# The last sums by pairs of experts, turned logits first, the last weight block in pieces, and the output's remainders in two transfers

## The chip, the cores and the metric

The kernel runs on one core of one Trainium2 chip. The metric is the time of one execution on the device, in microseconds (us); the figure for a kernel is the median of its runs. A profile shows one such execution: its span from the first instruction to the last, on TensorE (PE; its weight loads are PEld), VectorE (DVE), ScalarE (ACT), GpSimd (POOL) and SyncE (SP), whose queue issues nearly all transfers. The 16 DMA engines of the core move the data.

## The reference

Attention through a memory of 32 slots for each of 4 sequences and 8 heads, then a dense mixture of 4 experts, then a soft mixture of 8 experts with 4 slots each. The last part is where the change lies:

```python
def _moe_ref(x, domain_probs, w1, w2):
    p = domain_probs / (domain_probs.sum(-1, keepdims=True) + 1e-09)
    for e in range(E):                       # 4 experts, F = 1024
        h = np.maximum(x @ w1[e], 0.0)
        out += p[:, e:e + 1] * (h @ w2[e])

def _moe2_ref(x, phi, w1, w2):               # x: 2304 tokens x 512
    logits = x @ phi                         # 2304 x 32 slots
    d = np.exp(logits - logits.max(0)); d /= d.sum(0) + 1e-09
    slot_input = (d.T @ x).reshape(8, 4, 512)
    for e in range(8):                       # F = 1024
        h = np.maximum(slot_input[e] @ w1[e], 0.0)
        slot_out[e] = h @ w2[e]
    c = np.exp(logits - logits.max(1)); c /= c.sum(1) + 1e-09
    return c @ slot_out                      # 2304 x 512
```

## The kernel before

**The token part.** The 2304 tokens are worked in five units: three sequences of 576 tokens whole, the fourth in two halves of 288. In each unit `up` makes the hidden values of the four experts, 128 at a time, with three passes of matmuls (L767 to L769); ACT applies the relu (L776) into a ring of buffers `hts`, DVE turns them (L782), POOL multiplies them by the expert's share (L786). They stay in a large buffer `h` with regions R[0] to R[4] of 4608 words; in the last unit experts 0 and 1 lie in R[0] and experts 2 and 3 in R[1]. `w2` is not applied to tokens: the logits come from hidden values and a product `M` of `w2` and `phi` (L805, L812), and the slots' sums are taken over hidden values and multiplied by `w2` afterwards.

**The group behind each unit** (`group`). A matmul folds the four row groups of the logits (L922; in the last unit a second, L926). ACT copies the result from its PSUM bank to `lr` (L930, kept for the softmax over slots) and DVE turns the same bank into `lc` (L937). `lc` gives the running maximum (L946), the exponential (L951) and, turned back, `dt` (L957). Then the sums (L975): for each block `tb` of 32 tokens (9 in the last unit), each of the two pairs of experts `ep`, and each of four row groups `p`, one matmul with 32 rows, 32 columns and 512 streamed values. Its place in the array is row group `p` and column group `c = 2 * (tb % 2) + ep`; row group `p` writes bank `S0 + p`. Each fp32 matmul is two instructions, so the last unit has 72 matmuls in 144 instructions. DVE then adds them to the running sums, `srun` (L995).

**The end.** `srun` is turned (L1204), multiplied by the four `w2` (L1235), folded (L1249), and goes through the slot experts' `v1` (L1278) and `v2` (L1322). These weights are 40 blocks of 1 MB, `loads`: 8 of `w2`, 16 of `v1`, 16 of `v2`. Each gets a home in a part of a buffer that is no longer used (`homes`, 21 of them, in turn); the first 21 are issued as their homes come free, the other 19 each behind the block that held its home before. Five of the homes overlap R[0] and R[1], and two the buffers `hts`. SP issues them in program order, one at a time: an issue whose home is still read holds back all behind it. Each transfer also waits for the landing of the eighth before it. `load_block` issues a block as one transfer, or as two of 512 KB where its home has two parts.

The `v2` products of a half of the experts lie in one bank `ab`, in four column groups `kk`, 16 rows each. When the last block has been used, ACT and DVE copy the bank's halves (L1337, L1339), a matmul each (L1343) folds the four groups into banks `bf`, ACT and DVE copy these to `so4` (L1347, L1349), and `result` makes the output: matmuls (L1361), copies by DVE and ACT in turn (L1367, L1370), and transfers by SP (L365). The 64 tokens of each sequence beyond 512, its remainder, go out in four transfers of 128 KB from POOL's queue.

**The order.** Every step is handed to a planner with an engine, an estimated cost, what it reads and writes, and a due time `at`. The planner lists the steps of each engine in the order in which it believes they can start; that list is the program. Dependences and the waits for them are found per instruction when the program is built. Two engines' reads of one PSUM bank wait for one another, in program order.

## Time and profile before

| | us |
|---|---|
| median of 3 runs | 506.42 |
| lowest and highest run | 505.79, 507.36 |
| the profiled execution | 505.81 |
| its span, first to last instruction | 504.0 |
| PE busy in the span | 472.2 |
| DVE, ACT, POOL busy | 297.5, 202.4, 214.7 |

The granted TensorE clock is full up to the last microseconds (0.992 on average). PE is busy nearly without gaps from about 50 to 410 us. Behind that, in the last 94 us, the stages are short and have different limits: the DMA engines' share of time, the chain through PE, DVE and ACT, and SP's waits have to be read stage by stage, by windows of the trace and by the timeline. SP's waits are told with what released them, and a share of DMA time of 1 means that all 16 engines moved data throughout.

### The profile page before, as it was taken

To read this page: it belongs to the slowest core of one execution; us is meant where nothing else is said; L and a number is where in the kernel's file an instruction comes from. 1 tells how busy PE (TensorE), PEld (TensorE's weight loads), DVE (VectorE), ACT (ScalarE), POOL (GpSimd) and SP (SyncE) were. 2 spreads that over 40 slices of the span, in tenths; PEclk is the share of its full clock that TensorE was granted. 3 is DMA by queue.
4 is the path that set the end of the run, shared out by engine and by line. 5 is a ranking of instruction groups with operands and counts; after the bars stand their busy time and mean duration, and the time that the engine had idled before them with its cause. 6 is when DMAs were issued, how large, how long until landed. Compare 5 with 4: busy or idle time off the path is not lost.

```text
span 504.0 us, 13235 instructions
## 1 busy us (share of the span) xinstructions
PE 472.2 (94%) x5596; PEld 339.2 (67%) x5596; DVE 297.5 (59%) x606; ACT 202.4 (40%) x476; POOL 214.7 (43%) x259
## 2 busy tenths in 40 slices
PE   3889999999999999999999999999999989999880
PEld 2677678787886788788768887866697866332230
DVE  6588546657675958767875676685667553110041
ACT  2354345555551455455334655543452430010031
POOL 0244133646652347785315578643674950000001
PEclk9999999999999999999999999999999999999996
DMA  7999956416430847362073734643436998999948
GB/s 223 219 350 301 366 146 213 164 31 189 132 120 3 283 118 223 107 189 83 3 228 110 220 125 164 201 142 126 168 97 223 360 345 309 413 426 420 420 167 287
DMA packets 65403, 106.08 MB, mean 210 GB/s; under 512 B 28608, under 2 KB 40896, under 8 KB 59712
## 3 DMA queue, kind: packets, MB, share of 16 engines
q1 hardware_dynamic: 65152, 104.71, 61.3%
q8 instruction: 44, 0.72, 0.6%
q0 software_dynamic: 192, 0.52, 0.5%
q14 instruction: 15, 0.12, 0.1%
HBM read 100.50 MB, written 4.72 MB: 209 GB/s over the span
## 4 chain that ended last, share of the span: by engine, by line
PE 84%; DMA 7%; DVE 3%; SPq 2%; ACT 1%; issue 0%; DVEq 0%; ACTq 0%
PE ps L767 15%; PE ps L769 13%; PE ps L768 13%; PE ps L975 8%; PE ps L692 6%; PE ps L805 5%; DMA h<-in_moe_w_dram 5%; PE ps L1278 4%; PE ps L836 3%; SPq L365 2%; PE ps L600 2%; PE ps L612 2%; PE ps L1322 2%; PE ps L812 2%; PE ps L853 2%; DMA h<-in_q_dram 2%
## 5 line engine op out<-in xcount | busy, mean ns | idle before, releaser
L786 POOL TENSOR_TENSOR h<-h,pe 128x576 f32<-128x576 f32 (+1 forms) x160 | 158.0, 995 | 138.5 <-DVE h L782 108.4
L767 PE MATMUL ps<-A,g 128*128 128x288 f32 x512 | 157.9, 308 | 0.0
L776 ACT ACTIVATE hts<-ps 128x288 f32<-128x288 f32 x256 | 105.2, 412 | 130.6 <-PE ps L769 129.2
L769 PE MATMUL ps<-A,g 128*128 128x288 f32 x512 | 151.5, 296 | 0.2 <-DVE g L703 0.2
L768 PE MATMUL ps<-A,g 128*128 128x288 f32 x512 | 151.2, 295 | 0.0
L782 DVE STREAM_TRANSPOSE h<-hts 128x576 f32<-128x576 f32 (+1 forms) x160 | 102.8, 648 | 51.3 <-ACT hts L776 50.8
L767 PEld LDWEIGHTS ps<-A,g 128*128 128x128 f32 x512 | 96.3, 188 | 22.5 <-issue 14.2
L769 PEld LDWEIGHTS ps<-A,g 128*128 128x128 f32 x512 | 96.2, 188 | 0.9 <-DVE g L703 0.9
L768 PEld LDWEIGHTS ps<-A,g 128*128 128x128 f32 x512 | 96.4, 188 | 0.1
L703 DVE TENSOR_TENSOR g<-ps,g 128x512 fp32r<-128x512 f32 x64 | 41.0, 678 | 17.8 <-ACT g L701 17.7
L701 ACT CAST g<-ps 128x512 fp32r<-128x512 f32 x64 | 34.9, 590 | 33.8 <-PE ps L692 33.1
L975 PE MATMUL ps<-h,dts 32*32 32x512 f32 x1152 | 40.0, 597 | 1.6 <-DVE dts L957 1.6
L365 POOL DMA_DIRECT2D out_dram<-v x4 | 2.3, 568 | 80.2 <-ACT v L1370 80.2
L692 PE MATMUL ps<-raw,vbs 64*32 64x512 f32 x512 | 35.0, 601 | 1.3 <-DVE small L636 1.3
L975 PEld LDWEIGHTS ps<-h,dts 32*32 32x32 f32 x1152 | 22.8, 103 | 15.2 <-issue 4.7
L805 PE MATMUL ps<-hts,M 128*32 128x288 f32 x384 | 28.2, 411 | 0.0
L629 POOL TENSOR_TENSOR atts<-atts,small 128x256 f32<-128x256 f32 (+1 forms) x20 | 11.4, 572 | 25.2 <-DVE small L627 25.1
L836 PE MATMUL ps<-ident,h 128*128 128x128 f32 x128 | 18.1, 278 | 1.1 <-DMA h<-in_moe_w_dram 1.1
L805 PEld LDWEIGHTS ps<-hts,M 128*32 128x32 f32 x384 | 10.4, 109 | 10.6 <-issue 5.1
L640 POOL TENSOR_TENSOR atts<-atts,small 128x256 f32<-128x256 f32 (+1 forms) x20 | 11.5, 573 | 13.0 <-DVE small L638 5.5
L836 PEld LDWEIGHTS ps<-ident,h 128*128 128x128 f32 x128 | 14.5, 143 | 3.4 <-DVE h L782 1.4
L893 POOL TENSOR_TENSOR lts<-lts,pe 128x288 f32<-128x288 f32 x15 | 10.3, 688 | 13.0 <-DMA v<-in_moe_w_dram 9.6
(186 smaller groups left out, 519.0 us busy)
## 6 DMA issues: line engine op xcount, KB each, us to landing
raw<-in_moe_w_dram SPq DMA_DIRECT2D x32, 1024.0 KB, 5.3
v<-in_moe_w_dram SPq DMA_DIRECT2D x20, 1024.0 KB, 11.7
h<-in_moe_w_dram SPq DMA_DIRECT2D x18, 1024.0 KB, 8.2
h<-in_k_dram SPq DMA_DIRECT2D x8, 512.0 KB, 5.1
h<-in_v_dram SPq DMA_DIRECT2D x8, 512.0 KB, 6.5
atts<-in_moe_w_dram SPq DMA_DIRECT2D x4, 1024.0 KB, 9.2
atts<-in_q_dram SPq DMA_DIRECT2D x12, 256.0 KB, 5.7
atts<-in_phi_dram SPq DMA_DIRECT2D x8, 256.0 KB, 4.8
```

What stands on the lines that cost most here:

```text
L692: nc.tensor.matmul(bank[bs[c]][32 * i:32 * i + 32, :], vb[b % 2][64 * c:64 * c + 64, 32 * i:32 * i + 32], t()[64 * c:64 * c + 64, i, :], s ...
L701: add(ACT, act(512), lambda c=c, src=src: nc.scalar.copy(out=placed(g()[:, 2 * c]), in_=src), r=[pk(bs[c])], w=[wk(o + 1024 * c, 512)], at ...
L703: add(DVE, dve(512), lambda c=c, src=src: nc.vector.tensor_tensor(out=placed(g()[:, 2 * c + 1]), in0=src, in1=placed(g()[:, 2 * c].bitcast ...
L767: nc.tensor.matmul(t, gh, ah, start=(c == 0), stop=False)
L768: nc.tensor.matmul(t, gh, al, start=False, stop=False)
L769: nc.tensor.matmul(t, gl, ah, start=False, stop=(c == 1))
L776: add(ACT, act(w), lambda: nc.scalar.activation(out=t[:, o0 - base:o1 - base], in_=bank[bm][:, 0:w], func=ACTF.Relu,), r=[pk(bm)], w=[wk(h ...
L782: add(DVE, dve(width), lambda: nc.vector.transpose(out=h_of(u, e)[:, kx], in_=t), r=[wk(ho, width)], w=[hk], at=at + 0.4)
L786: add(POOL, pool(width), lambda: nc.gpsimd.tensor_tensor(out=h_of(u, e)[:, kx], in0=h_of(u, e)[:, kx], in1=share, op=ALU.mult), r=["pe"], ...
L805: nc.tensor.matmul(lb[r0:r0 + 32, 0:HB], M[:, 4 * n + a, :], at_place(hos[a] + o0, o1 - o0), start=(first and h == 0), stop=(not first and ...
L836: nc.tensor.transpose(bank[bk][:, 128 * c:128 * c + 128], wn()[:, a, 128 * c:128 * c + 128], ident)
L975: nc.tensor.matmul(bank[S0 + p][32 * c:32 * c + 32, :], dtv[rows, tb, :], h_pair(u, ep)[rows, :, :, tb, :], start=(tb < 2), stop=(tb >= nt ...
```

## The change

Six edits. (1) In every unit, DVE's turning of the folded logits into `lc` is put ahead of ACT's copy of them to `lr`. (2) In the last unit the sums run over all token blocks for experts 0 and 1 first and then for experts 2 and 3, where they took both pairs block by block; `c` keeps its formula. A home in R[0] so hangs on the first pair alone. (3) The last eight matmuls of the last unit's logits become seven and one. (4) The last `v2` block is issued in three transfers, of 512, 256 and 256 KB. Its last 128 rows are no longer multiplied into `ab` but, with a new 128-wide table `hl` that holds the hidden values of expert 7 at the columns of its slots four times over, straight into the banks `bf`, ahead of the fold. `hl` lies in the share table `pe`; POOL clears it and DVE fills it. (5) The output's remainders go out from SP in two transfers of 256 KB, two sequences each. (6) Some estimated costs and due times change with them.

```diff
@@ logits
-                for m, ho in enumerate(hos):
+                for m in ms:
...
-        add(PE, 1.1, f,
-            r=[("M", m) for m in range(n0, n + 1)] + [wk(o, width) for o in hos], w=[pk(LB)], at=at, lag=0)
+        last = u == NU - 1 and n == NCH - 1
+        for ms in (range(7), range(7, 8)) if last else (range(8),):
+            add(PE, 0.15 * len(ms) if last else 1.1, lambda ms=ms: f(ms),
...
@@ group
-        for ki, bk in enumerate((b1, b2)[:len(ranges)]):
-            add(ACT, act(HB), lambda ki=ki, bk=bk: nc.scalar.copy(
-                out=lr[:, HB * ki:HB * ki + HB], in_=bank[bk][:, 0:HB],
-            ), r=[pk(bk)], w=["lr"], at=at[0] + 0.1)
...
             add(DVE, dve(HB), lambda ki=ki, bk=bk: nc.vector.transpose(
                 out=lc[:, HB * ki:HB * ki + HB], in_=bank[bk][:, 0:HB],
             ), r=[pk(bk)], w=["lc"], at=at[0] + 0.1)
+        for ki, bk in enumerate((b1, b2)[:len(ranges)]):
+            add(ACT, act(HB), lambda ki=ki, bk=bk: nc.scalar.copy(
+                out=lr[:, HB * ki:HB * ki + HB], in_=bank[bk][:, 0:HB],
+            ), r=[pk(bk)], w=["lr"], at=at[0] + 0.2)
...
-        def sums(tbs):
+        def sums(tbs, eps):
             for tb in tbs:
-                for ep in range(2):
+                for ep in eps:
                     c = 2 * (tb % 2) + ep
                     for p in range(4):
...
-        for t0 in range(0, nt, 2):
...
+        for eps in ((0,), (1,)) if final else ((0, 1),):
+            ks = [hks[e] for e in range(E) if e // 2 in eps]
+            for t0 in range(0, nt, 2):
+                tbs = range(t0, min(t0 + 2, nt))
+                add(PE, 0.43 * len(tbs) + 0.02, lambda tbs=tbs, eps=eps: sums(tbs, eps), r=["dt"] + ks, w=sb, at=at[3])
@@ load_block
+            for a, z in ((0, 2), (2, 3), (3, 4)) if m == len(loads) - 1 else ((0, n),):
+                dma(
+                    lambda t=t, a=a, z=z, n=n: t() if z - a == n else t()[:, a:z],
+                    src if z - a == n else src[:, a:z], 262144 * (z - a), w=[wk(o + 512 * a, 512 * (z - a))],
...
@@ the end
+    hl = pe.rearrange("p b n e -> p (b n e)")[:, 0:128].rearrange("p (c s) -> p c s", c=4)
+    add(POOL, 0.3, lambda: nc.gpsimd.memset(hl, 0.0), w=["pe"], at=z4 + 2.4)
...
+            if m == 3:
+                nc.vector.tensor_copy(
+                    out=hl[:, :, 28:32], in_=tv[:, 1, 1, 3, 28:32].unsqueeze(1).to_broadcast([128, 4, 4])
+                )
...
+            for kks in ((0, 1), (2,)) if last else (range(4),):
+                add(PE, 0.15 * len(kks), lambda kks=kks, f=f: f(kks),
+                    r=[tk[kk] for kk in kks] + [("hz", e // 2)], w=[pk(ab)], at=at + 0.001 * kks[0])
...
         for h, cs in enumerate(halves):
+            if n:
+                add(PE, 0.45, lambda h=h, cs=cs, t=t: nc.tensor.matmul(
+                    bank[bf[h]][:, 0:256], hl.rearrange("p c s -> p (c s)"), t(3)[:, cs], start=False, stop=False,
+                ), r=[tk[3], "pe"], w=[pk(bf[h])], at=at + 0.09 + 0.1 * h)
             add(PE, 0.35, lambda n=n, h=h, so=so, fold=fold, cs=cs: nc.tensor.matmul(
...
-                dma(
-                    out[b * S + 512:b * S + 576, :], lambda t=t, b=b, rows_out=rows_out: t()[rows_out, b // 2, :],
-                    131072, r=[k_], w=[wk(o + 512 * b, 512)], at=at + 0.05, cost=1.0, eng=POOL,
-                )
                 at += 0.1
+                if b % 2:
+                    dma(
+                        out.rearrange("(b s) d -> b s d", b=B)[b - 1:b + 1, 512:576, :],
+                        lambda t=t, b=b: t()[:, b // 2, :], 262144, r=[k_, ("tail", b - 1)],
...
```

How this moves instructions, at three places. First SP's queue where the homes in `hts` and in R[0] and R[1] are loaded (`h_89` is that buffer; 128x2048 is a block of 1 MB, 128x1024 half of one; a wait names the engines or the transfers waited for). Before:

```order
L365 DMA hts<-in_moe_w_dram 128x2048 [waits DMAHW2_49,DVE_49,PE_49]
L365 DMA hts<-in_moe_w_dram 128x1024 [waits DMAHW3_49]
L365 DMA h_89<-in_moe_w_dram 128x1024 [waits DMAHW4_49,PE_49,Pool_49]
L365 DMA h_89<-in_moe_w_dram 128x2048 [waits DMAHW5_49]
L365 DMA h_89<-in_moe_w_dram 128x2048 [waits DMAHW6_49]
L365 DMA h_89<-in_moe_w_dram 128x2048 [waits DMAHW7_49]
L365 DMA h_89<-in_moe_w_dram 128x2048 [waits DMAHW0_49]
L365 DMA atts<-in_moe_w_dram 128x2048 [waits DMAHW1_49,PE_49]
```

And now:

```order
L365 DMA hts<-in_moe_w_dram 128x1024 [waits DMAHW2_49,DVE_49,PE_49]
L365 DMA hts<-in_moe_w_dram 128x2048 [waits DMAHW3_49,DVE_49,PE_49]
L365 DMA h_89<-in_moe_w_dram 128x2048 [waits DMAHW4_49,PE_49,Pool_49]
L365 DMA h_89<-in_moe_w_dram 128x2048 [waits DMAHW5_49,Pool_49]
L365 DMA h_89<-in_moe_w_dram 128x1024 [waits DMAHW6_49,PE_49,Pool_49]
L365 DMA h_89<-in_moe_w_dram 128x2048 [waits DMAHW7_49]
L365 DMA h_89<-in_moe_w_dram 128x2048 [waits DMAHW0_49]
L365 DMA atts<-in_moe_w_dram 128x2048 [waits DMAHW1_49,PE_49]
```

Two whole blocks, which wait for PE's first pair of experts, now stand ahead of the half block, which waits for the second pair.

Second, PE from the last `v2` block to the first results (L1322 and now L1340 are the `v2` matmuls, L1343 and now L1368 the folds). Before:

```order
L1322 MATMUL ps_92<-h_89,vbs 16x512 [waits DMAHW5_49]
L1322 MATMUL ps_92<-h_89,vbs 16x512 x3
L1343 MATMUL ps_99<-lrs,r_69 128x256 [waits Activation_49]
L1343 MATMUL ps_98<-lrs,r_69 128x256 [waits DVE_49]
L1361 MATMUL ps_93<-kbs,ct 128x256 [waits Activation_49]
L1361 MATMUL ps_94<-kbs,ct 128x256
L1361 MATMUL ps_95<-kbs,ct 128x256 [waits DVE_49]
```

And now:

```order
L1340 MATMUL ps_92<-h_89,vbs 16x512 [waits DMAHW5_49]
L1340 MATMUL ps_92<-h_89,vbs 16x512
L1340 MATMUL ps_92<-h_89,vbs 16x512 [waits DMAHW6_49]
L1365 MATMUL ps_99<-h_89,pe 128x256 [waits DMAHW7_49,Pool_49]
L1368 MATMUL ps_99<-lrs,r_69 128x256 [waits Activation_49]
L1365 MATMUL ps_98<-h_89,pe 128x256
L1368 MATMUL ps_98<-lrs,r_69 128x256 [waits DVE_49]
L1386 MATMUL ps_93<-kbs,ct 128x256 [waits Activation_49]
L1386 MATMUL ps_94<-kbs,ct 128x256
L1386 MATMUL ps_95<-kbs,ct 128x256 [waits DVE_49]
```

The block's four matmuls are now three, behind two transfers, and the third transfer is waited for by the first of two new matmuls, one ahead of each fold.

Third, SP's queue at the output. Before (the remainders are in POOL's queue):

```order
L365 DMA out_dram<-atts 128x1024 [waits DMAHW1_49,Activation_49]
L365 DMA out_dram<-h_89 128x512 [waits DMAHW2_49,DVE_49]
L365 DMA out_dram<-h_89 128x512 [waits DMAHW3_49,Activation_49]
L365 DMA out_dram<-h_89 128x1024 [waits DMAHW4_49,Activation_49]
L365 DMA out_dram<-h_89 128x1024 [waits DMAHW5_49,DVE_49]
L365 DMA out_dram<-atts 128x1024 [waits DMAHW6_49,Activation_49]
```

And now:

```order
L365 DMA out_dram<-atts 128x1024 [waits DMAHW3_49,Activation_49]
L365 DMA out_dram<-h_89 128x512 [waits DMAHW4_49,DVE_49]
L365 DMA out_dram<-h_89 128x512 [waits DMAHW5_49,Activation_49]
L365 DMA out_dram<-v 2x64x512 [waits DMAHW6_49,DVE_49,Activation_49]
L365 DMA out_dram<-v 2x64x512 [waits DMAHW7_49,DVE_49,Activation_49]
L365 DMA out_dram<-h_89 128x1024 [waits DMAHW0_49,DVE_49]
```

The two remainder transfers stand ahead of the last four of SP's transfers. At the split of the logits' last eight matmuls the order of PE's instructions is the same as before.

## Rows read from the trace of the kernel before

**Rows 1.** The page: mean busy share of the 16 DMA engines, 40 slices of 12.6 us.

```profile
DMA  7999956416430847362073734643436998999948
```

**Rows 2.** Windows behind the sums: stretch, its length, each engine's busy us (instructions), clock, DMA share, GB/s.

```profile
419.00:420.00 1.00, 1.00 (x30) 0.31 (x10) 0.00 (x0) 0.00 (x0) 0.00 (x0) 1.00 0.22 78
420.00:421.00 1.00, 1.00 (x12) 0.72 (x8) 0.67 (x2) 0.00 (x0) 0.00 (x0) 1.00 0.00 0
421.00:422.00 1.00, 0.81 (x8) 0.57 (x6) 1.00 (x4) 0.00 (x0) 0.00 (x0) 1.00 0.45 66
422.00:423.00 1.00, 0.56 (x5) 0.57 (x6) 1.00 (x3) 0.00 (x0) 0.00 (x0) 1.00 0.83 188
```

**Rows 3.** Timeline, 412 to 430: start us, us, engine, line, tiles, count [idle before <-releaser].

```profile
412.08 0.40 ACT L930 COPY lrs<-ps 128x288 f32<-128x288 f32 x1 [3.17 <-PE ps L926]
412.51 0.48 DVE L937 STREAM_TRANSPOSE lcs<-ps 128x288 f32<-128x288 f32 x1 [1.27 <-ACT lrs L930]
...
414.96 5.39 PE L975 MATMUL ps<-h,dts 32*32 32x512 f32 x144 [1.60 <-DVE dts L957]
...
420.49 2.63 SPq L365 DMA_DIRECT2D h<-in_moe_w_dram  x5
...
427.28 2.01 SPq L365 DMA_DIRECT2D atts<-in_moe_w_dram  x3
```

**Rows 4.** Windows of line L975 alone, start of its 144 instructions: PE, PEld busy us.

```profile
414.90:415.10 0.20, 0.14 (x16) 0.14 (x31) 1.00 0.77 328
```

**Rows 5.** Timeline of ACT and DVE at the third unit's group.

```profile
330.40 1.07 ACT L701 CAST g<-ps 128x512 fp32r<-128x512 f32 x2 [0.38 <-PE ps L692]
...
329.75 0.85 DVE L937 STREAM_TRANSPOSE lcs<-ps 128x288 f32<-128x288 f32 x2
...
331.55 1.28 DVE L703 TENSOR_TENSOR g<-ps,g 128x512 fp32r<-128x512 f32 x2
```

**Rows 6.** Timeline of PE at the `v2` blocks of experts 4 to 7.

```profile
467.29 1.05 PE L1322 MATMUL ps<-v,h 128*16 128x512 f32 x8
...
468.87 1.05 PE L1322 MATMUL ps<-v,h 128*16 128x512 f32 x8
...
480.71 1.05 PE L1322 MATMUL ps<-h,vbs 128*16 128x512 f32 x8 [0.86 <-DMA h<-in_moe_w_dram]
```

**Rows 7.** Timeline from the last block to the first and last outputs.

```profile
483.15 1.05 PE L1322 MATMUL ps<-h,vbs 128*16 128x512 f32 x8 [0.80 <-DMA h<-in_moe_w_dram]
484.27 0.37 ACT L1337 COPY lrs<-ps 128x256 f32<-128x256 f32 x1 [18.12 <-PE ps L1322]
484.68 0.42 DVE L1339 COPY lrs<-ps 128x256 f32<-128x256 f32 x1 [18.07 <-ACT lrs L1337]
...
484.69 1.16 PE L1343 MATMUL ps<-lrs,r 128*128 128x256 f32 x4 [0.49 <-ACT lrs L1337]
...
485.43 0.37 ACT L1347 COPY kbs<-ps 128x256 f32<-128x256 f32 x1 [0.79 <-PE ps L1343]
...
485.89 0.42 DVE L1349 COPY kbs<-ps 128x256 f32<-128x256 f32 x1 [0.79 <-PE ps L1343]
...
487.54 1.29 SPq L365 DMA_DIRECT2D out_dram<-h  x2
...
494.40 3.77 SPq L365 DMA_DIRECT2D out_dram<-atts  x2
```

**Rows 8.** Transfers by queue from 488 to 493: packets, MB, share of 16 engines.

```profile
q1 hardware_dynamic: 637, 1.70, 88.1%
```

**Rows 9.** The same from 493 to 499; POOL's transfers are the software queue.

```profile
q0 software_dynamic: 191, 0.52, 41.5%
```

**Rows 10.** Windows: loads of 512 KB, then the end of the output (columns as above).

```profile
473.00:477.00 4.00, 2.97 (x23) 1.03 (x24) 0.00 (x0) 0.00 (x0) 0.00 (x0) 1.00 1.03 419
...
501.00:502.00 1.00, 0.00 (x0) 0.00 (x0) 0.00 (x0) 0.00 (x0) 0.00 (x0) 0.50 0.68 279
502.00:503.00 1.00, 0.00 (x0) 0.00 (x0) 0.00 (x0) 0.00 (x0) 0.00 (x0) 0.50 0.13 53
```

More of the change, by code (lines that the diff above doesn't have):

```diff
@@ L796, in logits, with f @@
         hos = [ht_of[u, m, a] for m in range(n0, n + 1) for a in range(4)]
-        def f():
+        def f(ms=range(8)):
             if len(ranges) == 2:
@@ L810, in f @@
             else:
-                for m, ho in enumerate(hos):
+                for m in ms:
                     nc.tensor.matmul(
-                        lb[32 * (m % 4):32 * (m % 4) + 32, 0:HB], M[:, 4 * n0 + m, :], at_place(ho, HB),
+                        lb[32 * (m % 4):32 * (m % 4) + 32, 0:HB], M[:, 4 * n0 + m, :], at_place(hos[m], HB),
                         start=m < 4, stop=m >= 4,
@@ L816, in logits @@
         width = ranges[-1][1] - base
-        add(PE, 1.1, f,
-            r=[("M", m) for m in range(n0, n + 1)] + [wk(o, width) for o in hos], w=[pk(LB)], at=at, lag=0)
+        last = u == NU - 1 and n == NCH - 1
+        for ms in (range(7), range(7, 8)) if last else (range(8),):
+            add(PE, 0.15 * len(ms) if last else 1.1, lambda ms=ms: f(ms),
+                r=[("M", m) for m in range(n0, n + 1)] + [wk(o, width) for o in (hos[ms[0]:ms[-1] + 1] if last else hos)],
+                w=[pk(LB)], at=at + (0.01 * ms[0] if last else 0), lag=0)
     def m_chunk(n, ats):
@@ L978, in sums @@
                         )
-        for t0 in range(0, nt, 2):
-            tbs = range(t0, min(t0 + 2, nt))
-            add(PE, 0.43 * len(tbs) + 0.02, lambda tbs=tbs: sums(tbs), r=["dt"] + hks, w=sb, at=at[3])
+        for eps in ((0,), (1,)) if final else ((0, 1),):
[3 more added lines that the diff above has]
+                add(PE, 0.43 * len(tbs) + 0.02, lambda tbs=tbs, eps=eps: sums(tbs, eps), r=["dt"] + ks, w=sb, at=at[3])
         for p in range(4):
@@ L1305, in spread_h @@
                 )
-        add(DVE, 0.5, spread_h, r=[pk(bt)], w=[("hz", m)] + hzs[m][1], at=zz + 2.6)
+            if m == 3:
+                nc.vector.tensor_copy(
+                    out=hl[:, :, 28:32], in_=tv[:, 1, 1, 3, 28:32].unsqueeze(1).to_broadcast([128, 4, 4])
+                )
+        add(DVE, 0.6, spread_h, r=[pk(bt)], w=[("hz", m)] + hzs[m][1] + (["pe"] if m == 3 else []), at=zz + 2.6)
     so4 = kbs.rearrange("p n c x -> p (n c x)")
@@ L1318, in program, with f @@
             ab = accs[e // 4]
-            def f(e=e, nn=nn, t=t, ab=ab):
-                for kk in range(4):
+            last = (e, nn) == (7, 1)
+            def f(kks, e=e, nn=nn, t=t, ab=ab):
+                for kk in kks:
                     nc.tensor.matmul(
-                        bank[ab][32 * kk:32 * kk + 16, :], hz(e, nn, kk), t(kk),
-                        start=(e % 4 == 0 and nn == 0), stop=(e % 4 == 3 and nn == 1),
+                        bank[ab][32 * kk:32 * kk + 16, :], hz(e, nn, kk), t(kk), start=(e % 4 == 0 and nn == 0),
+                        stop=(e == 3 and nn == 1) or (e == 7 and nn == (0 if kk == 3 else 1)),
                     )
             at = zz + 0.1 * (2 * e + nn)
-            add(PE, 0.6, f, r=tk + [("hz", e // 2)], w=[pk(ab)], at=at)
+            for kks in ((0, 1), (2,)) if last else (range(4),):
+                add(PE, 0.15 * len(kks), lambda kks=kks, f=f: f(kks),
+                    r=[tk[kk] for kk in kks] + [("hz", e // 2)], w=[pk(ab)], at=at + 0.001 * kks[0])
             refill(at + 0.05)
@@ L1341, in program @@
         fold = (rr, r1)[n].rearrange("p i s -> p (i s)")
+        t, tk = blk[2, 7, 1]
         for h, cs in enumerate(halves):
+            if n:
+                add(PE, 0.45, lambda h=h, cs=cs, t=t: nc.tensor.matmul(
+                    bank[bf[h]][:, 0:256], hl.rearrange("p c s -> p (c s)"), t(3)[:, cs], start=False, stop=False,
+                ), r=[tk[3], "pe"], w=[pk(bf[h])], at=at + 0.09 + 0.1 * h)
             add(PE, 0.35, lambda n=n, h=h, so=so, fold=fold, cs=cs: nc.tensor.matmul(
@@ L1390, in program @@
                 )
-                dma(
-                    out[b * S + 512:b * S + 576, :], lambda t=t, b=b, rows_out=rows_out: t()[rows_out, b // 2, :],
-                    131072, r=[k_], w=[wk(o + 512 * b, 512)], at=at + 0.05, cost=1.0, eng=POOL,
-                )
                 at += 0.1
+                if b % 2:
+                    dma(
+                        out.rearrange("(b s) d -> b s d", b=B)[b - 1:b + 1, 512:576, :],
+                        lambda t=t, b=b: t()[:, b // 2, :], 262144, r=[k_, ("tail", b - 1)],
+                        w=[wk(o + 512 * (b // 2), 512)], at=at,
+                    )
             continue
```

2 lines of the change are left out of this document (1 added, 1 removed).

## Prediction

> **What bounds the kernel now.** I read the page's slices first, then windows of the last hundred microseconds, then the timeline at the places the change touches. The DMA engines are near full from the 32nd slice on, with an 8 in the 34th (415.8 to 428.4) and 4 and 8 in the last two [rows 1]. The reader should see two things in the windows behind the last token sums: DMA falls to 0.22, 0, 0.45 and 0.83 of full in four microseconds, 2.5 us of engine time lost [rows 2], and SP issues five loads at 420.49, right where the sums end, 414.96 + 5.39 = 420.35 [rows 3]. From there to the last weight block the engines are full, so what starts the loads sooner should end them sooner. PE does not set that end: it waits about 0.8 us for each of the last blocks, which come every 2.44 us (480.71, then 483.15), although it can do one in 1.58 us [rows 6, 7]. Behind the last block a chain of matmul, copies and folds runs 4.39 us to the first output [rows 7], and then 4.7 MB go out. So three stretches can pay: the hole, the chain, the output.
>
> **Turned logits first.** ACT's copy starts at 412.08 and DVE's turn of the same bank at 412.51 [rows 3]. With the turn first, everything from there to the sums comes 0.43 us sooner: -0.4. ACT's copy then lies beside DVE's next steps. In the four earlier groups ACT now waits for DVE. At the third unit DVE reaches the turns at 329.75 and does two in 0.85; ACT was free for its casts at 330.02 and got their matmuls at 330.40 [rows 5]. Now its second copy ends about 331.0, and the casts, queued behind it, come 0.6 later. The first, half of 1.07 and a little, ends at 331.6, where DVE wanted it at 331.55 [rows 5], and PE waits for DVE. That is 0.05. The other groups have no cast behind the copy. I take +0.1 and keep 0 to 0.7, one whole shift, for the range.
>
> **The sums by pairs.** The first 16 instructions run at once [rows 4]: each matmul has its own place, row group `p` and column group `c`. Two token blocks with both pairs fill the 16 places, so nine blocks are four and a half rounds, five turns of 5.39 / 5 = 1.08 us [rows 3]. One pair has only columns 0 and 2, or 1 and 3: eight places. Is a round of eight shorter? The nearest row is a `v2` block, a lone round of four places, and it takes 1.05 us [rows 6]: a round costs the same however many places it fills. So the first pair's nine blocks are again five turns, 5.39 us, and end no sooner than both pairs do now. The second pair's first two blocks can go beside the first pair's last one (other columns); its other seven take four turns more. The sums take 5.39 + 4 x 1.08 = 9.7 us. The other bound is 5.39, with the first pair done in half of it; I take 9.7, since four places and sixteen agree. No row shows whether a matmul may pass one that waits for its place. The Trainium skill (TensorE: Matmul & The Clock Gate, the mechanism of packing small matmuls) says that matmuls start and end strictly in program order; by that the turns add up as here, and without it the sum would be 5.39.
>
> What follows: the sums start at 414.53 and the first pair ends at 419.92, so the two whole blocks are issued at 420.06, where five loads were at 420.49. The gain is the 0.4 already counted, and the hole shrinks by that alone. The second pair ends at 424.23, so SP holds the half block, and all behind it, until 424.4. The two blocks are 2.1 MB, 5.0 us at 419 GB/s [rows 10], from about 421.3, so they last to 426.3; data follow an issue by 1 to 2 us (420.49 to the window 421 to 422 [rows 2, 3]). That is just in time. The next refills are released by PE's work on `w2`, at 427.28 [rows 3], 6.93 behind the sums; they move to 431.2, data by 432.2 to 433.2, and the 2.5 blocks ahead of them last to 432.5. PE as a whole is 3.9 us late. It catches up where it waits: from the block at 467.29 to that at 480.71 are six blocks in 13.42 us, which at 1.58 take 9.48 [rows 6], room for 3.94. All three fit with little to spare: +0.1, range 0 to 1.5.
>
> **The last block in pieces.** Bytes are the same. Rows become 4 and 2 KB; the nearest price is the output, 16 x 5 x 0.881 / 1.70 = 41.5 engine-us per MB [rows 8], against 16 x 1.03 / 0.419 = 39.3 for loads of half blocks [rows 10]: 0.5 MB of it is 0.07 us. Take +0.1. Call T the time at which PE sees the last landing, 483.15 now. Now ACT copies at T + 1.12, the folds' results are copied at T + 2.28 (ACT) and T + 2.74 (DVE), the first output starts at T + 4.39 [rows 7]. Then: the second piece lands 256 KB / 419 GB/s = 0.63 ahead, its matmul is through at T - 0.63 + 1.12 = T + 0.49, ACT's half is copied at T + 0.86 and DVE's, after it, at T + 1.32. On PE a matmul of 256 columns takes some 0.43 of the 1.16 for two folds with their drain. The new matmul runs before ACT is done, the first fold starts at T + 0.88, the second new matmul at 1.31, the second fold at 1.74. A copy follows 0.74 behind the start of its fold (484.69 to 485.43 [rows 7]): T + 1.62 and T + 2.48. The output needs both halves, and so comes 2.74 - 2.48 = 0.26 sooner. Net -0.2, range -0.5 to +0.2.
>
> **The remainders.** POOL's four transfers, 0.52 MB, took 41.5% of 16 engines for 6 us, 39.8 engine-us [rows 9]. At SP's price of 41.5 per MB the same bytes cost 21.6. The engines were full, so 18.2 / 16 = 1.1 us go. At the end they finish unevenly: 0.68 and 0.13 of full in the last two microseconds [rows 10], so they would end together 1.0 sooner than the last does. I take half of that as POOL's doing, where packets of two prices share the engines: -1.6 in all, range 0 to -2.1. SP's two more issues are hidden as long as the engines are behind it; they are, since the last issue begins near 496.3 and the end is over 6 us later [rows 7, 10].
>
> **At nothing.** The logits' split leaves PE's order as it was. The table's clearing is POOL's last step, the fill one small copy on DVE ahead of an idle stretch of 18 us [rows 7]; if that cover went, each would cost a few tenths.
>
> The sum: -0.4 + 0.1 + 0.1 - 0.2 - 1.6 = -2.0. The profiled execution took 505.81 (span 504.0 and 1.8 around it), so 503.8; it lies 0.6 below the median of the runs, 506.42, which gives 504.4.
>
> **The rivals.** (a) *The first pair frees its home early.* A round of eight places takes half a turn, the pair ends at 414.53 + 2.7 = 417.2, before the queue runs dry, and the hole of 2.5 goes whole. For it: the diff orders it so. Against it: the lone round of four [rows 6]. It gives 504.4 - 2.2 = 502.2. (b) *The longer sums are not covered.* The refills come 0.7 late, PE is 0.4 late at the last block, the casts cost 0.4: 505.9, no difference. For it: all margins are a few tenths. (c) *SP becomes the bound of the output.* Its last two issues took 1.9 us each [rows 7]; if that is their own price and not the engines' back-pressure, two more eat the 1.6: 506.0. (d) *The pieces pay one by one.* If each of the two further pieces began only when the one ahead had landed, each would add the way from issue to data, up to 1.9 us: 504.4 + 3.8 = 508.2, slower. It decides from 1.8 us a piece. Against it: halves of blocks in the same queue keep 419 GB/s [rows 10]. The Trainium skill (DMA: Bandwidth & Descriptors, the bandwidth measured by size) asks for transfers of 1 MiB and more, with about 2 us fixed in each; by that it would be 4.0 and 508.4, and rows 10 speak against it for transfers that queue behind others.
>
> **How the numbers follow.** Forecast 0.55, spread 503.4 to 505.4; (a) 0.10; (b) 0.20; (c) 0.08; (d) 0.07. Measurement can tell 0.3%, 1.5 us, from no change: faster means below 504.9. About four fifths of the forecast, all of (a) and a little of (b) lie there: 0.56. The rest of the forecast, (b) and (c) make 0.37, (d) 0.07. The range 502.1 to 506.1 leaves out (d) and the edges.
>
> **What would show it.** Right: the 144 instructions of the sums take near 9.7 us, the five loads start near 420.1, 420.5 and then 424.4; DMA's hole stays about 2 us; PE waits again for the last two blocks; the first output comes near T + 4.1; no software queue, and an even end of the output. Wrong: sums of 5.4 us, or loads issued before 418 (rival a); a second dip near 426 or 432, or PE without a wait for the last block (b); output with DMA below full before its end (c); a gap between the last three landings (d).

## The result, and the profile after

The changed kernel takes 513.75 us (median of 4 runs, 513.18 to 515.36) against 506.11 (4 runs, 505.04 to 507.36): 1.0147 times as long, 95% interval 1.0117 to 1.0176. I had forecast 504.4 and given slower a chance of 0.07, by another mechanism. The profiled execution took 515.36, with a span of 513.6. Executions differ from one another in their first 30 us, while the first inputs land, so I read stages from a row inside the kernel: here line L767 first runs at 32.3, in the kernel before at 29.5, and its last instruction is at 409.6 and 407.9.

Up to the output nothing was lost. The timeline from the last fold of the logits to the refills (line numbers have moved: L926 is L929, L937 is L936, L930 is L940, L975 is L978, L1322 is L1340):

```profile
412.95 0.75 PE L929 MATMUL ps<-lts,rr 128*128 128x288 f32 x2 [0.42 <-DVE lts L896]
...
413.74 0.48 DVE L936 STREAM_TRANSPOSE lcs<-ps 128x288 f32<-128x288 f32 x1 [0.84 <-PE ps L929]
414.26 0.40 ACT L940 COPY lrs<-ps 128x288 f32<-128x288 f32 x1 [3.68 <-DVE lcs L936]
...
416.19 7.39 PE L978 MATMUL ps<-h,dts 32*32 32x512 f32 x144 [1.17 <-DVE dts L960]
...
420.78 4.24 SPq L365 DMA_DIRECT2D h<-in_moe_w_dram  x5
...
430.51 1.19 SPq L365 DMA_DIRECT2D atts<-in_moe_w_dram  x2
```

DVE turns before ACT copies. The sums take 7.39 us where they took 5.39, and SP issues the first load 4.59 behind their start, where it was 5.53 [rows 3]. Only the two whole blocks come sooner. The half block and the two loads behind it wait for PE's second pair, as the prediction had said: the third of the five is issued at 423.72, 7.53 behind the start of the sums, where in the kernel before it is at 421.35, 6.39 behind. Both issues, the changed kernel's first, and the changed kernel's wait for them on SP between 421.5 and 426 (us, times, longest):

```profile
423.72 0.33 SPq L365 DMA_DIRECT2D h<-in_moe_w_dram  x1
421.35 0.42 SPq L365 DMA_DIRECT2D h<-in_moe_w_dram  x1
SPq L365 <- PE ps L978: 1.4, 1, 1.4
```

The DMA hole is shallow now; to compare with [rows 2] (columns as there):

```profile
420.00:421.00 1.00, 1.00 (x36) 0.43 (x25) 0.00 (x0) 0.00 (x0) 0.00 (x0) 1.00 0.90 369
421.00:422.00 1.00, 1.00 (x25) 0.55 (x17) 0.00 (x0) 0.00 (x0) 0.00 (x0) 1.00 0.61 123
422.00:423.00 1.00, 1.00 (x31) 0.47 (x15) 0.00 (x0) 0.00 (x0) 0.00 (x0) 1.00 0.75 188
423.00:424.00 1.00, 1.00 (x18) 0.49 (x5) 0.43 (x2) 0.00 (x0) 0.00 (x0) 1.00 0.79 319
```

That is 0.95 us of engine time lost in four microseconds instead of 2.5. The timeline from the last block to the output, against [rows 7]:

```profile
483.36 1.32 PE L1340 MATMUL ps<-h,vbs 128*16 128x512 f32 x6
484.61 0.70 PE L1365 MATMUL ps<-h,pe 128*128 128x256 f32 x2
...
486.74 0.42 DVE L1374 COPY kbs<-ps 128x256 f32<-128x256 f32 x1 [1.20 <-PE ps L1368]
...
488.40 1.57 SPq L365 DMA_DIRECT2D out_dram<-h  x2
490.06 0.88 SPq L365 DMA_DIRECT2D out_dram<-atts  x2
491.03 2.18 SPq L365 DMA_DIRECT2D out_dram<-h  x2
493.31 1.47 SPq L365 DMA_DIRECT2D out_dram<-v  x2
494.88 5.20 SPq L365 DMA_DIRECT2D out_dram<-h  x2
500.17 1.61 SPq L365 DMA_DIRECT2D out_dram<-atts  x2
```

Counted from the last fold, the first output starts at 75.45 (412.95 to 488.40), where it was 76.25: 0.8 sooner. The fold in the kernel before:

```profile
411.29 0.75 PE L926 MATMUL ps<-lts,rr 128*128 128x288 f32 x2 [0.43 <-DVE lts L893]
```

The loss begins behind the first output. Windows of the output:

```profile
490.00:495.00 5.00, 3.30 (x24) 1.20 (x16) 4.34 (x8) 3.58 (x7) 0.00 (x0) 1.00 0.93 359
495.00:500.00 5.00, 0.00 (x0) 0.00 (x0) 0.00 (x0) 0.00 (x0) 0.00 (x0) 0.52 0.44 135
500.00:505.00 5.00, 0.00 (x0) 0.00 (x0) 0.00 (x0) 0.00 (x0) 0.00 (x0) 0.50 0.87 322
505.00:512.00 7.00, 0.00 (x0) 0.00 (x0) 0.00 (x0) 0.00 (x0) 0.00 (x0) 0.50 0.14 55
```

For the last seven microseconds the DMA engines are busy to 0.14, at 55 GB/s. Of 16 engines two are 0.125. Behind the first output SP's longest wait is now the landing of the last one, at the end of the program (us, times, longest):

```profile
SPq L1458 <- DMA out_dram<-atts: 10.7, 1, 10.7
```

The remainders (`out_dram<-v`, 493.31) are the only new thing there. Their pattern on the output's side is 2 sequences x 64 rows x 512, the two sequences outermost, and on the side of SBUF 128 partitions.

### The profile page after: what moved, and what is told of

Read it like the earlier page. It is cut to its first block, busy times and chain, and to the rows that moved or that the text cites. A ratio compares the mean times of both kernels' runs of the same rounds, so it can differ in the third digit from the quotient of the medians.

```text
span 513.6 us, 13246 instructions
## 1 busy us (share of the span) xinstructions
PE 478.0 (93%) x5598; PEld 341.7 (67%) x5598; DVE 297.6 (58%) x607; ACT 202.6 (39%) x476; POOL 212.6 (41%) x256
## 4 chain that ended last, share of the span: by engine, by line
PE 85%; DMA 6%; DVE 2%; SPq 1%; ACT 1%; issue 0%; DVEq 0%; ACTq 0%
PE ps L767 15%; PE ps L769 13%; PE ps L768 13%; PE ps L978 8%; PE ps L692 6%; PE ps L805 5%; PE ps L1290 4%; DMA h<-in_moe_w_dram 3%; PE ps L839 3%; PE ps L600 2%; PE ps L612 2%; DMA h<-in_q_dram 2%; PE ps L812 2%; PE ps L856 2%; SPq L365 1%; PE ps L1245 1%
## 5 line engine op out<-in xcount | busy, mean ns | idle before, releaser
L767 PE MATMUL ps<-A,g 128*128 128x288 f32 x512 | 157.8, 308 | 0.0
L767 PEld LDWEIGHTS ps<-A,g 128*128 128x128 f32 x512 | 96.3, 188 | 22.5 <-issue 14.2
L978 PE MATMUL ps<-h,dts 32*32 32x512 f32 x1152 | 42.0, 596 | 1.2 <-DVE dts L960 1.2
L978 PEld LDWEIGHTS ps<-h,dts 32*32 32x32 f32 x1152 | 23.3, 103 | 16.2 <-issue 6.8
L839 PEld LDWEIGHTS ps<-ident,h 128*128 128x128 f32 x128 | 14.6, 143 | 2.1 <-issue 0.9
L654 POOL TENSOR_TENSOR A<-atts,A 128x256 fp32r<-128x256 f32 (+1 forms) x20 | 13.6, 678 | 4.4 <-ACT A L652 4.4
```

The lines of the kernel that those rows point to most:

```text
L767: nc.tensor.matmul(t, gh, ah, start=(c == 0), stop=False)
L839: nc.tensor.transpose(bank[bk][:, 128 * c:128 * c + 128], wn()[:, a, 128 * c:128 * c + 128], ident)
L978: nc.tensor.matmul(bank[S0 + p][32 * c:32 * c + 32, :], dtv[rows, tb, :], h_pair(u, ep)[rows, :, :, tb, :], start=(tb < 2), stop=(tb >= nt ...
```

## The experiments

"First load" and "first output" are counted from the start of the last unit's sums; "output" is from SP's first issue to the last packet; all four are of the profiled execution. A ratio is to runs of the kernel before that were taken beside that kernel's, with medians between 505.65 and 506.11, so it does not follow from the column of times. The last unit's steps up to the output are the same in changed, a_pool, a_tokens and a_one2, and their first outputs still lie between 71.4 and 72.2; c_adj, which differs in one column number, has 72.7. So a difference of less than about 1 us in that column tells nothing. l_copyfirst's is late by an event told below.

| kernel | us | ratio to before (95%) | sums | first load | first output | output |
|---|---|---|---|---|---|---|
| before | 506.11 | 1 | 5.39 | 5.53 | 72.6 | 15.2 |
| changed | 513.75 | 1.0147 (1.0117 to 1.0176) | 7.39 | 4.59 | 72.2 | 23.8 |
| a_pool | 505.83 | 1.0008 (0.9981 to 1.0035) | 7.39 | 4.59 | 72.0 | 15.1 |
| a_tokens | 504.89 | 0.9971 (0.9947 to 0.9995) | 7.39 | 4.60 | 71.4 | 14.6 |
| a_one2 | 510.08 | 1.0099 (1.0063 to 1.0136) | 7.39 | 4.59 | 72.0 | 19.3 |
| b_two2 | 514.21 | 1.0165 (1.0149 to 1.0180) | 5.39 | 5.54 | 73.1 | 23.5 |
| l_oldsums | 504.94 | 0.9971 (0.9958 to 0.9985) | 5.39 | 5.54 | 72.5 | 14.6 |
| l_oneblock | 505.13 | 0.9991 (0.9968 to 1.0013) | 7.39 | 4.59 | 72.3 | 14.8 |
| l_copyfirst | 505.02 | 0.9992 (0.9971 to 1.0013) | 7.39 | 4.59 | 73.1 | 14.5 |
| b_tokens | 505.97 | 0.9996 (0.9985 to 1.0007) | 5.39 | 5.53 | 72.6 | 14.6 |
| c_adj | 505.17 | 0.9993 (0.9981 to 1.0004) | 7.39 | 4.59 | 72.7 | 14.6 |
| c_four | 503.04, one run | | 5.98 | 3.27 | 70.7 | 14.5 |
| s_skew2 | 505.18 | 0.9990 (0.9974 to 1.0007) | 6.05 | 5.18 | 73.0 | 14.5 |
| s_skew4 | 505.08 | 0.9984 (0.9969 to 0.9999) | 6.71 | 4.99 | 72.2 | 14.8 |

### Where the loss lies

**a_pool** takes the fifth edit back:

```diff
-                if b % 2:
-                    dma(out.rearrange("(b s) d -> b s d", b=B)[b - 1:b + 1, 512:576, :], ...
+                dma(out[b * S + 512:b * S + 576, :], ..., 131072, ..., eng=POOL)
```

> The changed kernel with its fifth edit undone: the remainders again go out from POOL's queue, four transfers of 128 KB. Theory (two engines): the loss lies in the two transfers of 256 KB, which run on 2 of the 16 DMA engines; without them the first output still starts 0.8 us sooner than before (488.40 less the 1.66 that the profiled execution was late from its first 30 us, against 487.54), so 506.1 - 0.8 = 505.3, between 504.3 and 506.3, and the last 20 us look as in the kernel before. Rival (another edit): if the pair order or the pieces cost the time, it stays above 511. Rival (more issues on SP): as the theory here, near 505.

505.83: the loss is gone, so it lies in the two transfers and nowhere else. (Edits 1 to 4 without the fifth gain nothing that the times show: the interval contains 1.) **a_tokens** keeps them, two of 256 KB from SP, and only changes which dimension is outermost; the rows of two sequences lie beside one another in 64 partitions:

```diff
-                        out.rearrange("(b s) d -> b s d", b=B)[b - 1:b + 1, 512:576, :],
-                        lambda t=t, b=b: t()[:, b // 2, :], 262144, ...
+                        out.rearrange("(b s) d -> s b d", b=B)[512:576, b - 1:b + 1, :],
+                        lambda t=t, b=b: t()[0:64, b - 1:b + 1, :], 262144, ...
```

> The changed kernel with the remainders still in two transfers of 256 KB from SP, but with the tokens as the outermost dimension on both sides (64 partitions, each with two sequences of 2 KB rows), instead of the two sequences. Theory (two engines): the transfers spread over 16 engines, no queue of two remains; 505.3 less the 1.1 to 1.6 that I had put on the cheaper packets: 503.7 to 504.5. Rival (SP is the bound of the output: each issue it makes there costs 1 to 4 us): the same number of issues and bytes, so 512 or more. Rival (another edit): above 511.

504.89, 9 us less than the changed kernel with as many issues and bytes, though 0.4 above the range that I had expected. So it is neither SP's issues nor the size, but the pattern. **a_one2** writes sequences 0 and 1 as the changed kernel does and 2 and 3 as a_tokens:

```diff
+                if b == 1: dma(out.rearrange("(b s) d -> b s d", b=B)[0:2, 512:576, :], lambda t=t: t()[:, 0, :], ...
+                if b == 3: dma(out.rearrange("(b s) d -> s b d", b=B)[512:576, 2:4, :], lambda t=t: t()[0:64, 2:4, :], ...
```

> The changed kernel with one of the two remainder transfers as it is (sequences 0 and 1 outermost) and the other with the tokens outermost. Theory (two engines): on the two engines the transfer is 64 packets of 2 KB each at 84 ns, 5.4 us; one of two is gone and 0.7 us comes back as that engine's share of the spread one, so 513.75 - 4.7 = 509.0, between 508 and 510, and the last 5 us run with DMA at 0.13 of full. Rival (SP is the bound): 512 or more. Rival (another edit): above 511.

510.08, between the two: 5.2 for the first such transfer, 3.7 for the second by the medians, and 4.7 and 4.5 by the output's length (14.6, 19.3, 23.8). **b_two2** puts the two transfers alone, the fifth edit of the diff as it stands, into the kernel before:

> The kernel before with the fifth edit alone: the remainders from SP in the two transfers of 256 KB with the two sequences outermost. Theory (two engines): the two engines carry 10.8 us more than the others, and 506.1 becomes 513.5 to 515.5, with DMA at 0.13 of full for the last 6 to 8 us. Rival (another edit makes the loss): 504 to 506.5.

514.21, as expected. How many engines took part can be counted. Each transfer ends with a packet of 4 bytes on every engine that it used, and rows are 2 and 4 KB, so the packets under 512 B are these. The packet lines of 484 to 514 us, of the changed kernel, of a_one2 and of a_tokens:

```profile
DMA packets 1701, 4.74 MB, mean 158 GB/s; under 512 B 164, under 2 KB 164, under 8 KB 1700
```

```profile
DMA packets 1715, 4.74 MB, mean 158 GB/s; under 512 B 178, under 2 KB 178, under 8 KB 1714
```

```profile
DMA packets 1729, 4.74 MB, mean 158 GB/s; under 512 B 192, under 2 KB 192, under 8 KB 1728
```

192 is 12 transfers by 16 engines. Each transfer with the sequences outermost takes 14 away: it ran on two engines. In the changed kernel each of the two engines then has 2 x 128 KB more than the others, 64 packets of 2 KB per transfer at 84 ns (the median of the 2 KB packets in the last seven microseconds), 10.8 us in all, and its share of the four transfers behind them. The Trainium skill (DMA: Bandwidth & Descriptors, on why a DMA increments its semaphore by 16 and not by 1) says that a transfer runs on the largest number of engines up to 16 that divides the slowest dimension of both sides that is not 1. For 128 and 2 that is two, for 64 and 64 it is 16; the counts agree with both.

### What the other edits are worth

From here the base is a_tokens, the mended kernel. Each of three kernels takes one edit back from it; the fourth is the kernel before with the mended transfers. **l_oldsums**:

```diff
-        for eps in ((0,), (1,)) if final else ((0, 1),):
+        for eps in ((0, 1),):
```

> The kernel with the tokens outermost in the remainders (call it the mended one, 504.9), and its second edit undone: the sums take both pairs block by block again. In the mended one the sums start at 414.19, SP's first load of a home in R[0] is issued 4.60 behind, and the first output 71.42 behind; in the kernel before the loads are 5.53 and the output 72.58 behind. Theory: the pair order frees the first homes 0.9 us sooner, and that is most of the 1.16 between them; here the sums take 5.4 again, the output starts 72.2 to 72.4 behind them, and the time is 505.6 to 505.9. Rival (the prediction's: longer sums eat it): 71.4 behind, 504.9 or less.

The output starts 72.5 behind the sums, near my theory, but the 0.2 that its range spans cannot be told in this column, and the time is 504.94, no more than the mended kernel's. The pair order's 0.9 us at the first load is not seen in the time; three loads that come about 1 us later stand against the two that come sooner. **l_oneblock**:

```diff
-            for a, z in ((0, 2), (2, 3), (3, 4)) if m == len(loads) - 1 else ((0, n),):
+            for a, z in ((0, n),):
...
-            last = (e, nn) == (7, 1)
+            last = False
```

> The mended kernel with its fourth edit undone: the last weight block in one transfer, all its rows through the bank of the experts. Theory (as predicted): 0.2 to 0.3 us between the last landing and the first output, so the output starts 71.6 to 71.7 behind the start of the sums, and 505.1. Rival (the pieces carry most of the 1.16): 72.4 behind, 505.9. Rival (the pieces cost as transfers of their own): 71.0 behind, 504.5.

The output starts 72.3 behind the sums, where the rival had put it and not my theory, but that column cannot tell 0.7 us. Counted from the last byte of weights it can be told. By the packets, that byte lands 4.87 us ahead of the first output here and in the kernel before, and 4.57 to 4.66 in the kernels with pieces (but for l_copyfirst's execution, told next): the pieces give 0.2 to 0.3. The time, 505.13, is not told apart from 504.89. **l_copyfirst** puts ACT's copy back ahead of DVE's turn:

```diff
+        for ki, bk in enumerate((b1, b2)[:len(ranges)]):
+            add(ACT, act(HB), ... nc.scalar.copy(out=lr[...], in_=bank[bk][:, 0:HB]), ..., at=at[0] + 0.1)
             add(DVE, dve(HB), ... nc.vector.transpose(out=lc[...], ...
-            add(ACT, act(HB), ... nc.scalar.copy(...), at=at[0] + 0.2)
```

> The mended kernel with its first edit undone: ACT copies the folded logits before DVE turns them. Theory: 0.43 us more between the last fold of the logits on PE and the sums, 3.67 instead of 3.24; the first output is as much later, 505.3. Rival (the engines' queue of loads hides it): the output starts as early, counted from the fold, 504.9.

The sums start 3.67 behind the last fold and not 3.24, as predicted; the time, 505.02, doesn't tell it. Its profiled execution shows something else. Windows of the same columns:

```profile
430.00:436.00 6.00, 6.00 (x64) 1.70 (x54) 2.81 (x8) 0.44 (x1) 0.00 (x0) 1.00 1.01 422
436.00:439.00 3.00, 2.30 (x16) 1.80 (x8) 0.00 (x0) 0.58 (x1) 0.00 (x0) 0.96 1.01 425
439.00:446.00 7.00, 6.62 (x26) 1.59 (x27) 0.29 (x1) 0.00 (x0) 0.00 (x0) 0.53 1.02 421
446.00:455.00 9.00, 9.00 (x68) 3.02 (x66) 1.26 (x4) 1.37 (x2) 0.00 (x0) 1.00 1.01 420
```

The same stage in a_tokens' execution, which lies 2.0 us earlier:

```profile
434.00:437.00 3.00, 2.29 (x16) 1.83 (x8) 0.00 (x0) 0.59 (x1) 0.00 (x0) 1.00 1.02 430
437.00:444.00 7.00, 6.62 (x53) 2.21 (x57) 0.33 (x2) 0.69 (x1) 0.00 (x0) 1.00 1.02 420
```

In both PE idles for 0.7 of three microseconds. Behind it the granted clock is 0.53 for seven (1.2 GHz for nearly all of them) in the one and full in the other. The changed kernel's own execution lies between:

```profile
440.00:447.00 7.00, 7.00 (x48) 1.93 (x48) 0.00 (x0) 0.24 (x1) 0.00 (x0) 0.76 1.02 421
```

Of the 14 profiled executions of the table, all with that idle stretch, five keep the full clock behind it, eight have 0.76 over seven microseconds, with either order of the sums, and l_copyfirst's alone 0.53. Its fall costs PE some 3 us (7 x 0.47), and with the 2 us that the pair order has already spent, PE no longer waits for any of the last blocks; the first output comes 5.9 us behind the last byte, 1.3 more than in the mended kernel. So PE can become the bound: my rival (b), in a single execution. With 0.76 the margin is just used up in the changed kernel and in a_one2: PE waits for none of the last blocks either, and the output still comes 4.6 to 4.7 behind the last byte.

**b_tokens** is the kernel before with the lines of a_tokens for the remainders, the fifth edit alone and mended:

> The kernel before with the remainders in two transfers from SP, tokens outermost, and nothing else. Theory: the price that the prediction put on this edit, with all 16 engines at work: 1.1 to 1.6 us less, 504.4 to 504.9, the output's last landing 14.0 to 14.5 us behind the first issue where it was 15.6. Rival (POOL's packets cost nothing that counts): 506.

505.97 to 505.9: nothing, the rival. In the profile the output is 0.6 shorter, less than the 1.1 to 1.6 I had priced. Windows of the output in a_tokens say why:

```profile
486.00:492.00 6.00, 4.51 (x30) 1.41 (x24) 5.32 (x9) 4.63 (x9) 0.00 (x0) 1.00 0.90 345
492.00:495.00 3.00, 0.00 (x0) 0.00 (x0) 0.00 (x0) 0.00 (x0) 0.00 (x0) 0.80 0.98 208
495.00:500.00 5.00, 0.00 (x0) 0.00 (x0) 0.00 (x0) 0.00 (x0) 0.00 (x0) 0.50 0.99 404
```

While the remainders go out, the engines are as busy as behind them and move half as much: 208 GB/s at 0.98 against 404 at 0.99. That is 47 engine-us for 0.62 MB, 75 per MB; POOL's 39.8 for 0.52 [rows 9] are 76. Both read 64 partitions, where the other outputs read 128; that this is the reason I did not test. Packets of 2 KB alone are not: those of the changed kernel, from 128 partitions, take 84 ns, 41 per MB.

### What sets the length of the sums

The changed kernel starts a new round of eight instructions every 0.43 us, as this window view of L978 alone shows (PE and PEld busy, instructions in it; an instruction that lasts into the next window counts in both):

```profile
416.18:416.58 0.40, 0.39 (x8) 0.18 (x16) 1.00 1.21 512
416.58:417.00 0.42, 0.42 (x16) 0.16 (x8) 1.00 0.82 341
```

Eight run and sixteen weights are loaded. **c_adj** moves a pair's two column groups next to one another; **c_four** gives each pair all four:

```diff
-                    c = 2 * (tb % 2) + ep
+                    c = 2 * ep + tb % 2
```

```diff
-                    c = 2 * (tb % 2) + ep
+                    c = tb % 4 if final else 2 * (tb % 2) + ep
```

> The mended kernel with one line of the sums changed, so that the two token blocks of a turn and one pair of experts lie in neighbouring column groups (c = 2 * ep + tb % 2 where c was 2 * (tb % 2) + ep), and the folding matrix that takes the columns together to match. In the changed kernel a new round of eight instructions, one token block of one pair, starts every 0.43 us, although the next block has other columns. Theory (a turn is one block of one pair, whatever its columns): the sums take 7.4 again, the first home's load is issued 4.6 behind their start, the time stays at 504.9. Rival (neighbouring columns run beside one another, as the two pairs of a block did in the kernel before: 16 instructions within 0.11 us): a pair takes 2.7, the sums 5.4, the first load is issued 2.8 behind the start of the sums, and the time falls by 1 to 2 us.

> The mended kernel with the last unit's sums spread over all four column groups for each pair (c = tb % 4); the two pairs are then added into the same places, so the sums of the last unit are mixed, and only the times count. Theory (a turn is one block of one pair): 7.4 again or 7.7, without the overlap of the pairs' ends. Rival (my prediction's: places decide, and a pair with all 16 places runs in four and a half rounds of 16): the first pair ends in half the time, near 2.7, and the sums take 5.4.

Timelines of c_adj and of c_four, and the first window of L978 in each:

```profile
414.36 7.39 PE L978 MATMUL ps<-h,dts 32*32 32x512 f32 x144 [1.18 <-DVE dts L960]
...
418.95 4.32 SPq L365 DMA_DIRECT2D h<-in_moe_w_dram  x5
```

```profile
414.57 5.98 PE L978 MATMUL ps<-h,dts 32*32 32x512 f32 x144 [1.18 <-DVE dts L960]
...
417.84 4.34 SPq L365 DMA_DIRECT2D h<-in_moe_w_dram  x5
```

```profile
414.35:414.75 0.40, 0.39 (x8) 0.18 (x16) 1.00 0.97 410
414.56:414.96 0.40, 0.39 (x16) 0.24 (x32) 1.00 0.92 389
```

Which two columns makes no difference; four instead of two do. With four, 16 instructions run and 32 weights are loaded, and the pair frees its home at 3.27 and not at 4.60. The theory of c_four (a block is a turn, whatever its columns) falls; its rival was right in kind, if too low in both numbers. Its one run, 503.04, is below every run of every other kernel here, but it adds both pairs into the same places; a kernel that frees the home so soon and keeps the pairs apart was not run, so what that would be worth stays open.

What is a round of eight? A matmul is two instructions. The first fold L1343 of the kernel before fills the whole array, and of its two instructions one runs for 0.32 us while the weights of both are loaded. A `v2` block is four matmuls on four places; four of its eight instructions run first, with all eight weights loaded, and the other four start 0.44 us behind them. First windows of both, in the kernel before:

```profile
484.69:485.01 0.32, 0.32 (x1) 0.30 (x2) 1.00 0.00 0
467.28:467.70 0.42, 0.41 (x4) 0.13 (x8) 1.00 0.89 371
```

Read in the same way, a round of eight is the first instructions of eight matmuls, two token blocks on eight places, and the next round their second ones. The trace does not name the places, but c_adj and c_four bear this out: their first two blocks lie in the same column groups, 0 and 1, and yet eight instructions start at once in the one and 16 in the other, which rounds of one block each would not give. So a place takes its next block after two rounds, 0.86 us, where eight places are in use, and after 1.08 [rows 3] where all 16 are.

**s_skew2** and **s_skew4** let the first pair lead by two and by four blocks and alternate behind that:

```diff
+            turns = [((i - 2 * ep,), (ep,)) for i in range(nt + 2) for ep in range(2) if 0 <= i - 2 * ep < nt]
```

> The mended kernel with another order of the last sums: experts 0 and 1 lead by two token blocks, and behind them the blocks of the two pairs alternate, so that both pairs are in the array for most of the time. Measured so far: block by block 5.39 with the first home's load 5.54 behind the start, pair by pair 7.39 with 4.60. Theory (a column group takes its next block 0.86 after the last when two of the four are in use, and 1.08 when all are): pair 0 ends between 4.7 and 5.2 behind the start, the sums take 5.8 to 6.3, PE keeps 1.1 to 1.6 us of the slack that the pair order spends, and the time is 504.3 to 504.9. Rival (the sums' order has no bearing on the time): 504.9 as both others. Rival (instructions of the two pairs wait for one another in program order): 7.4 or more and 505.

> As the last, with a lead of four token blocks. Theory: pair 0 ends between 4.6 and 4.9 behind the start, the sums take 6.3 to 6.8, and the time is 504.3 to 504.9, less even from run to run than with a lead of two, since PE is the later the longer the lead. Rivals as there.

The sums take 6.05 and 6.71 and the first load comes at 5.18 and 4.99: the sizes fit, and the pairs do not hold one another up. The times, 505.18 and 505.08, are above the 504.3 to 504.9 that I had expected and again don't move; and the runs with a lead of four are closer together (504.25 to 507.15) than those with two (503.94 to 508.83), where I had expected the reverse. Five orders of the same sums (l_oldsums, a_tokens, c_adj and these two), with the first load between 4.59 and 5.54, lie between 504.89 and 505.18.

## Why the prediction was wrong, point by point

**The remainders** are the step that failed, twice over. I priced the two transfers by bytes, "at SP's price of 41.5 per MB", and so took it for granted that they spread over the 16 engines as SP's other outputs do. They ran on two. Instead of -1.6 the edit was worth +8.2 (b_two2, 514.21 against 505.99), and no bound of the range, 0 to -2.1, allowed for a loss. The pattern stood in the diff: "b s d" has a 2 outermost, while every transfer behind my price had 128. The second error is smaller: spread over 16 engines, the remainders still move at half of the others' rate, so the -1.1 for cheaper packets does not exist (b_tokens: no gain in the time, 0.6 in the profile, about the 0.5 that I had put on an even end).

**The sums by pairs** were mis-sized. Predicted: 9.7 us, the first pair through at 5.39, the loads sooner by the 0.4 of the turned logits alone, and a hole of about 2. Measured: 7.39, the first load 0.94 sooner than before against the sums' start, and a hole of 0.95. The step that failed is the turn of 1.08 us "however many places it fills", which rested on a lone block of four places [rows 6]. That block's 1.05 runs from its first start to its last end, and the 1.08 from one turn's start to the next; that they agree says nothing of a turn of eight places, which takes 0.86. Four such turns and the 1.05 of a last block alone are 4.5, and the first pair is through at about 4.45 (4.59 less the 0.14 between the end of the sums and SP's issue in [rows 3]). The overlap was too small as well: twice 4.45 is 8.9, and the two pairs together take 7.39, so they overlap by 1.5 and not by one turn. What I had said of the half block held: it waits for the second pair, 7.53 behind the start of the sums (predicted 9.9, with the longer sums). The rule of the Trainium skill that I had weighed there (TensorE: Matmul & The Clock Gate, the packing of small matmuls: starts and ends strictly in program order) speaks, as I read it, for turns that add up; this trace does not agree.

**Turned logits first**: predicted -0.4, measured 3.24 for 3.67 from the last fold to the sums, and the +0.1 for the earlier groups does not show: from the first to the last instruction of L767 it is 377.3 to 378.4 us over the executions with the turn first and 377.5 to 378.4 over the others.

**The last block in pieces**: predicted -0.2, range -0.5 to +0.2; measured -0.2 to -0.3 from the last byte to the first output, not seen in the time.

**The rivals.** (a) came true in part: the first pair is through at 4.45 and not at 2.7 behind the start of the sums, and the hole shrinks from 2.5 to 0.95 without going whole; the order that comes near it is c_four's. (b), the longer sums not covered, is what l_copyfirst's execution shows, at a slow clock. Its sign, PE without a wait for the last blocks, shows in the changed kernel too, but costs nothing there. (c), SP as the bound of the output, falls with a_tokens: the two issues that take 5.20 at 494.88 take 2.25 there, with as many ahead of them. (d), the one that ended slower, is not what happened: one block or three pieces, the output starts within 0.3 us of the same distance from the last byte, and in a_tokens the last three landings are 0.63 and 0.64 apart, no more than 256 KB take at 419 GB/s. Slower came from a mechanism that I had not listed.

**The sum.** With the pattern mended, the kernel takes 504.89 where I had said 504.4, 0.29% faster than the kernel before. The profiles show -0.43, -0.3 and -0.6 for three edits and up to -0.9 for the pair order at the first load; together that would be over 2, and the medians show 1.1. Part of the rest is lost ahead of the output: from the last fold to the first output, the kernels whose steps up to there are the old ones (before, b_two2, b_tokens) take 76.2 to 76.7 us, and those with the edits (changed, a_pool, a_tokens, a_one2, c_adj) 74.7 to 75.9. The means differ by 1.1, of which the first and the fourth edit have 0.7. So some 0.4 is left for the pair order, less than one execution differs from the next; l_oldsums, without it, has 75.8. The 0.6 of the output is not seen in the times (b_tokens). Where that goes is not settled. The pair order's cost, 2 us of PE's slack, is seen only when the clock falls. l_oldsums, without it, is as fast (504.94), and its 12 runs lie closest together, 504.10 to 505.39, which may be chance. It is the version that I would keep; it and a_tokens are 0.3% faster than the kernel before, by intervals that end short of 1.

## What to carry to other kernels

Before a transfer is priced by its bytes, look at the outermost dimension of both of its sides and count the engines that it will run on; the same 256 KB cost 4.5 us more on two engines than on 16, and in one queue everything behind them waits for the two. The price of a packet is taken from a transfer that reads as many partitions, and a small matmul's from a row with as many column groups in use. An order that brings one wait 0.9 us forward is to be judged by all that hang on it: here three loads came about 1 us later, and PE's slack was gone in the execution with the lowest clock. And a time from first start to last end is not the time after which the next may start.

## What the runs showed of the hardware

- A transfer with two sequences outermost runs on two of 16 engines: 14 completion packets fewer each, and 55 GB/s for both engines together while they work alone.
- 0.5 MB of output from 64 partitions moves at 208 GB/s with the engines busy to 0.98, against 404 from 128.
- Of small fp32 matmuls in 32x32 places, eight instructions start every 0.43 us with two column groups in use; with all four, 16 start at a time and 32 in 1.08 us. Which two columns makes no difference (7.39 us for the sums either way).
- Behind the same stretch, in which PE idled for 0.7 us, the granted clock over the next seven microseconds was 1.00 in five executions, 0.76 in eight and 0.53 in one. What decides it these runs don't tell.
